# Two memory chains and a feed-forward layer on one core: where the feed-forward pieces stand, a lag of 6 in place of 8, and weights that stay in SBUF

## Chip, cores, metric

One core of one Trainium2 chip. The metric is the device time of one execution in microseconds (us), the median over several executions. The kernels were run in sets, each beside the kernel before on the same chip.

## The reference

Four layers on a sequence of 2048 rows of 448: attention with a carried memory (A), a gated feed-forward layer (B), A again, B again.

```python
x = x + A(layernorm(x));  x = x + B(layernorm(x))
x = x + A(layernorm(x));  x = x + B(layernorm(x))

# A: 64 segments of 32 rows, one after the other
for s in range(64):
    h = concat([mem, xs])                    # 8 memory rows + 32 rows
    q, k, v = h Wq, h Wk, h Wv               # 16 heads of 256
    p = softmax(mask(q k^T / 16))
    o = (p v) Wo
    mem, out = o[:8], o[8:]                  # the memory rows go to the next segment
# B: relu(x Wgate) * (x Wup), then Wdown; inner width 1792
```

The memory makes A serial: 64 segments, each after the other. The kernel runs the two A layers as two chains, the second LAG segments behind the first. One pass of the loop is a **step**: one segment of each chain. Steps in which only one chain runs are single steps, the others double. Both B layers are cut into tiles of 128 rows (four segments), 16 per chain.

## The kernel before

Wq Wk^T and Wv Wo are multiplied out per head at the start (M_sb, B_sb). A step is then: M product (G), scores with a mask, softmax, three value products, attention, and the turn of eight memory rows per chain into the next step's input. Parts (cuts marked):

```python
LAG = 8
# --- in a step: mask, half of the scores, mask, half of the scores
for bb in range(2):
    nc.tensor.matmul(S_ps[RR, bb, 0:8 * L], ident[RR, RR], maskbB[RR, :, :], start=True, ...)
    for sl in range(NSL):
        for c in chains:
            ...  nc.tensor.matmul(o, q_T, rhs, start=False, ...)
# ... softmax, value products, attention into AT_ps ...
# --- memory rows of both chains: ScalarE, then a copy on GpSimd, then five small transposes
for c in chains:
    nc.scalar.copy(mb[m_lo:m_hi, 0:DM], AT_ps[m_lo:m_hi, 0:DM])
    nc.gpsimd.tensor_copy(mb[m_lo:m_hi, 512:576], mb[m_lo:m_hi, 384:448])
    for kd in range(NSL):
        nc.tensor.transpose(MT_ps[:, kd, :], mb[m_lo:m_hi, lo:lo + 128], ...)
    set_memT(c, MT_ps[:, :, :], s + 1)

# --- layer norm: 12 small VectorE operations (Newton) for 1/sqrt, ScalarE scales
# --- feed-forward: tiles of both chains as a pair (N=256); weights come by DMA for each pair
for i, f in enumerate(range(f_lo, f_hi)):
    load_dm_rows(nc.sync if i % 2 == 0 else nc.gpsimd, wg, B_W_gate[:, f * 128:(f + 1) * 128])
    ...
# --- and stands in four chunks at the ends of steps
add_fill(base + 1, lambda pair=pair: ffn_chunk(pair, 0))
add_fill(base + 2, lambda pair=pair: ffn_chunk(pair, 1))
...
for g in range(nsteps):
    chain_step(g, chains, vox_tiles)
    for fn in fill[g]: fn()
```

## Time and profile before

| | |
|---|---|
| device time, 4 runs | 2062.09 us (2057.74 to 2063.97) |
| steps | 8 single, 56 double, 8 single |
| TensorE busy | 93% of the span |
| mean granted TensorE clock | 0.979 |
| read from HBM | 64.92 MB |

Four double steps and the feed-forward work of one pair make a **block**, some 115 us, and the kernel before spends 1610 us in 14 of them: the block is the thing to read.

### The profile page before, as it was taken

To read this page: it belongs to the slowest core of one execution; us is meant where nothing else is said; L and a number is where in the kernel's file an instruction comes from. 1 tells how busy PE (TensorE), PEld (TensorE's weight loads), DVE (VectorE), ACT (ScalarE), POOL (GpSimd) and SP (SyncE) were. 2 spreads that over 40 slices of the span, in tenths; PEclk is the share of its full clock that TensorE was granted. 3 is DMA by queue.
4 is the path that set the end of the run, shared out by engine and by line. 5 is a ranking of instruction groups with operands and counts; after the bars stand their busy time and mean duration, and the time that the engine had idled before them with its cause. 6 is when DMAs were issued, how large, how long until landed. Compare 5 with 4: busy or idle time off the path is not lost.

```text
span 2058.8 us, 79459 instructions
## 1 busy us (share of the span) xinstructions
PE 1916.8 (93%) x35590; PEld 1429.8 (69%) x35590; DVE 1237.5 (60%) x3406; ACT 663.5 (32%) x1429; POOL 457.8 (22%) x1223
## 2 busy tenths in 40 slices
PE   4799999999999999999999999999999999999997
PEld 1377777776767776676767776676767676776764
DVE  3645656666665656656665656656665656665543
ACT  2423332333333332333333332333333332333232
POOL 1201331121303130131303130131303130132232
PEclk9899999999999999999999999999999999999998
DMA  9500210020202020020102020020102020011121
GB/s 257 107 5 21 48 47 21 23 49 20 50 9 52 16 56 16 20 52 20 47 9 54 16 54 18 20 51 20 47 7 56 14 54 15 22 48 28 42 56 42
DMA packets 199541, 82.91 MB, mean 40 GB/s; under 512 B 177120, under 2 KB 191136, under 8 KB 199200
## 3 DMA queue, kind: packets, MB, share of 16 engines
q1 hardware_dynamic: 168240, 43.04, 9.4%
q0 software_dynamic: 20160, 28.93, 5.5%
q10 hardware_dynamic: 10800, 5.86, 1.0%
q8 instruction: 278, 4.55, 0.9%
q14 instruction: 63, 0.52, 0.1%
HBM read 64.92 MB, written 1.84 MB: 32 GB/s over the span
## 4 chain that ended last, share of the span: by engine, by line
PE 83%; DVE 8%; ACT 4%; issue 2%; DMA 1%; POOL 0%; SPq 0%; POOLq 0%; ACTq 0%; DVEq 0%
PE ps L255 30%; PE ps L379 22%; PE AT_ps L455 6%; PE gps L322 5%; PE ups L322 5%; PE S_ps L407 4%; PE dps L334 4%; ACT mb L465 2%; PE bps L115 2%; PE PT_ps L441 1%; PE MT_ps L470 1%; DVE G L390 1%; DVE x_ring L475 1%; ACT xn L218 1%; DVE stats L191 1%
## 5 line engine op out<-in xcount | busy, mean ns | idle before, releaser
L379 PE MATMUL ps<-hT,M_sb 128*128 128x80 bf16 (+1 forms) x16128 | 558.2, 198 | 19.8 <-DVE hT L241 18.1
L379 PEld LDWEIGHTS <-M_sb 128*128 128x128 bf16 x16128 | 555.2, 100 | 25.9 <-issue 22.0
L255 PE MATMUL ps<-B_sb,hT 128*32 128x448 bf16 x8192 | 419.8, 353 | 0.0
L255 PEld LDWEIGHTS <-hT 128*32 128x32 bf16 x8192 | 268.5, 96 | 114.7
L265 DVE CAST vox<-ps 128x448 bf16<-128x448 f32 x512 | 300.4, 620 | 41.8 <-PE ps L255 16.5
L390 DVE CAST G<-ps 128x160 bf16<-128x160 f32 (+1 forms) x312 | 184.7, 595 | 219.1 <-PE ps L379 218.9
L388 ACT CAST G<-ps 128x480 bf16<-128x480 f32 (+1 forms) x328 | 178.6, 549 | 390.3 <-PE ps L379 390.3
L466 POOL COPY mb<-mb 8x64 bf16<-8x64 bf16 x126 | 29.1, 231 | 1108.0 <-ACT mb L465 1108.0
L255 PE MATMUL ps<-B_sb,memT_padP 128*32 128x448 bf16 x4608 | 239.8, 353 | 0.0
L255 PEld LDWEIGHTS <-memT_padP 128*32 128x32 bf16 x4608 | 145.0, 96 | 69.0
L263 ACT CAST VOm<-ps 128x448 bf16<-128x448 f32 x288 | 139.9, 528 | 162.7 <-PE ps L255 162.5
L327 DVE SCALAR_TENSOR_TENSOR hh<-gps,ut 128x128 bf16<-128x128 f32 x448 | 111.9, 286 | 133.8 <-ACT ut L325 131.8
L322 PE MATMUL gps<-xnT,wg 128*128 128x256 bf16 (+1 forms) x1008 | 153.6, 275 | 18.4 <-DVE xnT L313 13.3
L465 ACT CAST mb<-AT_ps 8x448 bf16<-8x448 f32 x126 | 65.9, 523 | 286.0 <-PE AT_ps L455 284.7
L475 DVE TENSOR_TENSOR x_ring<-AT_ps,x_ring 32x448 bf16<-32x448 f32 x128 | 79.1, 618 | 122.5 <-ACT mb L465 118.7
L322 PE MATMUL ups<-xnT,wu 128*128 128x256 bf16 (+1 forms) x1008 | 148.8, 273 | 1.3 <-DMA wu<-in_B_W_up_dram 1.1
L325 ACT CAST ut<-ups 128x256 bf16<-128x256 f32 (+1 forms) x252 | 87.8, 348 | 155.1 <-PE ups L322 147.1
L407 PE MATMUL S_ps<-G,hT 128*40 128x320 bf16 (+1 forms) x1280 | 104.5, 275 | 19.2 <-ACT G L388 19.2
L413 DVE TENSOR_REDUCE mx<-S_ps 104x16 f32<-104x640 f32 (+1 forms) x72 | 59.3, 824 | 103.5 <-PE S_ps L407 103.5
L322 PEld LDWEIGHTS <-wg 128*128 128x128 bf16 x1008 | 93.4, 102 | 33.6 <-issue 19.6
L322 PEld LDWEIGHTS <-wu 128*128 128x128 bf16 x1008 | 96.6, 103 | 15.4 <-DMA wu<-in_B_W_up_dram 1.3
L455 PEld LDWEIGHTS <-PT 128*40 128x40 bf16 x1024 | 54.8, 99 | 75.0 <-issue 39.8
(80 smaller groups left out, 1942.0 us busy)
## 6 DMA issues: line engine op xcount, KB each, us to landing
wg<-in_B_W_gate_dram SPq DMA_DIRECT2D x126, 96.0 KB, 2.5
wu<-in_B_W_up_dram SPq DMA_DIRECT2D x126, 96.0 KB, 2.5
wu<-in_B_W_up_dram POOLq DMA_DIRECT2D x126, 96.0 KB, 2.7
wg<-in_B_W_gate_dram POOLq DMA_DIRECT2D x126, 96.0 KB, 3.0
wo<-in_A_Wo_dram ACTq DMA_DIRECT2D x4, 896.0 KB, 6.5
wg<-in_B_W_gate_dram SPq DMA_DIRECT2D x126, 16.0 KB, 2.4
wu<-in_B_W_up_dram SPq DMA_DIRECT2D x126, 16.0 KB, 2.6
wu<-in_B_W_up_dram POOLq DMA_DIRECT2D x126, 16.0 KB, 2.5
```

The lines of the kernel that those rows point to most:

```text
L255: nc.tensor.matmul(ps[32 * hq:32 * hq + 32, 0:DM], lhsT_fn(kd), B_sb[:, kd, h * DM:(h + 1) * DM], start=(kd == 0), stop=(kd == KDT - 1), t ...
L263: nc.scalar.copy(dst[:, g, :], ps[:, 0:DM])
L265: nc.vector.tensor_copy(dst[:, g, :], ps[:, 0:DM])
L322: nc.tensor.matmul(ps[:, 0:N2], W_sb[:, kd, :], pair.xnT2[:, kd, 0:N2], start=(kd == 0), stop=(kd == KDT - 1))
L327: nc.vector.scalar_tensor_tensor(out=task.hh[:, f, :], in0=gps[:, 128 * i:128 * (i + 1)], scalar=0.0, in1=ut[:, 128 * i:128 * (i + 1)], op ...
L379: nc.tensor.matmul(ps[:, mi * NP:(mi + 1) * NP], M_sb[:, kd, (t0 + mi) * 128:(t0 + mi + 1) * 128], hTP[:, j, kd, c_lo:c_lo + NP], start=(k ...
L388: nc.scalar.copy(dst, src)
L390: nc.vector.tensor_copy(dst, src)
L407: nc.tensor.matmul(o, q_T, rhs, start=False, stop=(sl == NSL - 1), tile_position=(0, c.rb), skip_group_check=True)
L455: nc.tensor.matmul(at_tiles[c.cid][c.rb:c.rb + L, 0:DM], PT[:, gg, c.rb:c.rb + L], rhs, start=(gg == 0), stop=(gg == 7), tile_position=(0, ...
L465: nc.scalar.copy(mb[m_lo:m_hi, 0:DM], AT_ps[m_lo:m_hi, 0:DM])
L475: nc.vector.tensor_tensor(xrows, AT_ps[c.rb:c.rb + SEG, 0:DM], xrows, op=ALU.add)
```

## The change

The intent: keep TensorE occupied in the waits of a step, and drop steps, reloads and side work.

- Feed-forward per tile (N=128), cut into pieces (turn, seven gate-and-up products of 16 matmuls, down), in a queue; hooks put pieces after the M product (mid), before chain 2's value product (late), before the memory transposes (end) and after them (post).
- LAG 6: 70 steps, 12 single and 58 double.
- Gate and up weights loaded once. Tails of the 448-wide contraction share 128-row tiles, which frees the room for it.
- Both masks ahead of the scores; memory rows of chain 2 leave through VectorE while ScalarE does chain 1's.
- 1/sqrt of the layer norm by an addition and a power on GpSimd; the scaling after it moves from ScalarE to VectorE.
- Loads of wo, Wd and x moved to SyncE's queue.

The core of the diff, cut:

```diff
-LAG = 8
+LAG = 6
 ...
-            nc.scalar.dma_start(wo[:], WoF[:, 8 * i:8 * (i + 1), :])
+            nc.sync.dma_start(wo[:], WoF[:, 8 * i:8 * (i + 1), :])
 ...
+    for i, w in enumerate((B_W_gate, B_W_up)):
+        nc.sync.dma_start(Wgu[:, :, i, :], w[0:384].rearrange("(k p) n -> p k n", p=P))
+        nc.sync.dma_start(WguT[64 * i:64 * i + 64, :], w[384:448])
 ...
-        for _ in range(3):                       # Newton, on VectorE
-            ...
+        nc.gpsimd.tensor_scalar(out=rstd[:], in0=mv[:, 1:2], scalar1=EPS, scalar2=None, op0=ALU.add)
+        nc.gpsimd.tensor_tensor(out=rstd[:], in0=rstd[:], in1=mhalf[:], op=ALU.pow)
 ...
+        mid()
         for bb in range(2):
             nc.tensor.matmul(S_ps[RR, bb, 0:8 * L], ident[RR, RR], ...)
+        for bb in range(2):
             r4 = slice(4 * bb, 4 * bb + 4)
             ...
-                nc.scalar.copy(mb[m_lo:m_hi, 0:DM], AT_ps[m_lo:m_hi, 0:DM])
-                nc.gpsimd.tensor_copy(mb[m_lo:m_hi, 512:576], mb[m_lo:m_hi, 384:448])
+            (cp_a if c is chains[0] else cp_v)(mb[rows, 0:DM], at[c.cid][rows, 0:DM])
+        end()
         ...                                      # memory transposes
+        post()
 ...
+        if r == 0:                               # r: step number modulo 4
+            def mid():
+                fill(0, 3)
+            def end():
+                prep_ln(C1, gb + 2)
+                fill(0, 1)
+            def post():
+                fill(0, 1)
 ...
```

## The prediction

> **What bounds the kernel now.** I read the page's busy table first, then its chain of work, then a table of windows over the steady part, then the TensorE timeline of that part.
>
> ```profile
> span 2058.8 us, 79459 instructions
> PE 1916.8 (93%) x35590; PEld 1429.8 (69%) x35590; DVE 1237.5 (60%) x3406; ACT 663.5 (32%) x1429; POOL 457.8 (22%) x1223
> ...
> PE 83%; DVE 8%; ACT 4%; issue 2%; DMA 1%; POOL 0%; SPq 0%; POOLq 0%; ACTq 0%; DVEq 0%
> ```
>
> TensorE is busy 93% of the span and carries 83% of the chain that ended last. So two things count: how much TensorE work there is, and the 7% where it stands. The kernel has 72 steps: eight with chain 1 alone, 56 with both chains, eight with chain 2 alone. Four double steps and one pair of feed-forward tiles make a block; a typical one by windows (columns: length, then PE, PEld, DVE, ACT, POOL busy, clock, DMA share, GB/s):
>
> ```profile
> 906.00:1022.08 116.08, 110.74 (x2047) 83.56 (x2046) 73.02 (x206) 37.33 (x79) 25.32 (x69) 0.99 0.13 32
> ```
>
> TensorE stands 5.3 us in 116.1; no other engine is over two thirds busy. The timeline of one double step, with two later waits:
>
> ```profile
> 1027.21 8.19 PE L379 MATMUL ps<-hT,M_sb 128*128 128x80 bf16 x224
> 1035.33 0.73 PE L407 MATMUL S_ps<-G,hT 128*40 128x320 bf16 x10
> ...
> 1036.91 3.25 PE L255 MATMUL ps<-B_sb,memT_padP 128*32 128x448 bf16 x64
> 1039.95 3.24 PE L255 MATMUL ps<-B_sb,hT 128*32 128x448 bf16 x64
> 1043.12 0.36 PE L441 MATMUL PT_ps<-ident,Px 104*128 104x104 bf16 x4
> ...
> 1043.59 3.25 PE L255 MATMUL ps<-B_sb,hT 128*32 128x448 bf16 x64
> 1046.77 1.19 PE L455 MATMUL AT_ps<-vox,PT 128*40 128x448 bf16 x8
> ...
> 1049.21 0.80 PE L470 MATMUL MT_ps<-ident,mb 8*128 8x8 bf16 x9 [0.23 <-ACT mb L465]
> ...
> 1051.79 8.19 PE L379 MATMUL ps<-hT,M_sb 128*128 128x80 bf16 x224 [1.17 <-DVE hT L241]
> ...
> 1062.62 0.73 PE L407 MATMUL S_ps<-G,hT 128*40 128x320 bf16 x10 [1.73 <-ACT G L388]
> ```
>
> Differences of starts give the true cost, because durations overlap: M product 8.12, scores 1.58, two value products 6.21, transposes of P 0.47, third value product 3.18, attention 1.87, mask and memory transposes about 1.15. Sum 22.6 us of TensorE work per double step. The same reading of a single step (starts at 118.85 and 136.21 of the M product, 17.36 apart, waits 0.67 and 0.39 and their latencies taken off) gives 16.1.
>
> **What the Trainium skill says.** "TensorE: Matmul & The Clock Gate", section "Wait — 56ns, not 53.3ns?": warm matmuls start N/2.4 + 2.5 ns apart, 55.6 ns at N=128. Its section "Back-to-back issue gap" instead says about 81 ns at N=128 where each has its own weight load. It matters, because the change halves N in the gate and up products. The trace has N=128 groups of four, each with its own weights:
>
> ```profile
> 2038.20 0.63 PE L322 MATMUL gps<-xnT,wg 128*128 128x128 bf16 x4
> 2038.62 0.63 PE L322 MATMUL ups<-xnT,wu 128*128 128x128 bf16 x4
> ...
> 2041.16 0.39 PE L322 MATMUL ups<-xnT,wu 128*128 128x128 bf16 x4
> 2041.38 0.39 PE L322 MATMUL gps<-xnT,wg 128*128 128x128 bf16 x4
> ...
> 2045.66 0.34 PE L322 MATMUL ups<-xnT,wu 128*128 128x128 bf16 x3 [0.90 <-DMA wu<-in_B_W_up_dram]
> ```
>
> Starts 0.22 us apart per four: 56 ns, so the first section holds and the 81 do not. The 0.42 per four at 2038 is the cold clock of that page's section "What you observe": about half rate for some 3.4 us after idleness; here it lasted from 2037.4 to 2040.2. "DMA: Bandwidth & Descriptors", "Latency and other measured facts", gives 261 GB/s for a DMA transpose; here one of 0.92 MB held the queue for 3.9 us, 235 GB/s. "GPSIMD Engine Reference", "Elementwise — side-by-side cycle accounting", has two-input work on GpSimd about twice as slow as on VectorE; the change puts the power of the layer norm there, and no row of this trace has that operation.
>
> **The change part by part.** It is a rewrite; I built it and read its instruction order.
>
> *Unchanged.* The contraction of 448 still takes four matmuls: the tails of two heads now share a 128-row tile that meets a zeroed half of the input. That frees memory, not TensorE time. 224 + 64 + 64 (+64) matmuls per step stay.
>
> *Added on TensorE.* Gate and up run per tile at N=128. One pair before: 14 x 2 x 0.436 = 12.2 us; after: 2 x 14 x 2 x 0.223 = 12.5. Down stays 2.65 per tile. With 0.35 of transposes a tile costs 9.26.
>
> *Removed off the path.* The reload of gate and up weights for each of 18 pairs (GpSimd's and SyncE's queues) and 12 Newton operations of about 0.155 us per layer norm on VectorE. They free engines that were not the bound; their worth is in the waits.
>
> *Moved: the fillers.* Before, feed-forward work stood only at the ends of steps, in large chunks. Now pieces of 16 matmuls (0.89 us) stand after the M product (covers the eviction of G, the 1.73), between attention and the memory transposes (covers the mb eviction), and after these (covers the hT copies, the 1.17). The built order shows them there in three of four steps, and a down product of 2.65 in the fourth. VectorE's order has the x_ring addition of chain 1 ahead of the hT copies, so PSUM frees in time.
>
> *Fewer steps.* A lag of 6 gives 12 single and 58 double steps: content 12 x 16.1 + 58 x 22.6 = 1504 against 16 x 16.1 + 56 x 22.6 = 1523. 19 us of TensorE work less, and four partly empty single steps less.
>
> Now the clock from start to end, in us.
> - Start: first M product at 100.6 before. The first weight product began at 21.4 because two wo loads, Wd and x competed with the first transposes (10.1 and 7.2 us on the queue instead of 3.9). All these now follow in SyncE's queue: about 12. Twelve transposes of 3.9, four wo loads of about 3.8 and Wd of 6.6 make it load-bound: I walk the queue to a last product near 81, against 89. The 11.6 us that followed (layer norm, mem0, weights) shrink: both layer norms are scheduled early; the zeroing of the 16-slot input ring on GpSimd remains, 3.5 in all. Start 84.5.
> - Six single steps: four of 17.4, two with content 16.1, one feed-forward tile 9.3, transposes 1.1, leftover waits 0.5: 112.7. At 197.
> - 58 double steps: 58 x 22.6 = 1309 (22.58 unrounded), 27.7 feed-forward tiles x 9.26 = 256.5, 27 input transposes x 0.37 = 10: 1575.5. A block before had content 109.1 and took 116.1: 5.3 gaps and 1.7 of slower clock and tails. I leave 2.0 and 1.0 of these per block, x 14.5 = 43.5. Sum 1619. At 1816.
> - Six single steps: 96.6, two tiles and a down product 21.2, transposes 1.2, waits 3: 122. At 1938.
> - Last tile alone: before, 2030.7 to 2058.8, with the gate and up products stretched from 6.3 to 14 us by weight loads (the 0.90 above). After: addition 0.9, layer norm 2.4, turn 1.5, products cold at first 7.6, last eviction and down 3, addition 0.9, store 2.4: 18.7. At 1957.
>
> Device times lie about 2 us over the span (2060.7 for the profiled 2058.8): **1959 us**, 5% faster.
>
> **Rivals.** (1) *The waits move instead of going.* For it: in the second step of each block a down product, an addition, statistics, GpSimd's two operations and the scaling must run in 5 us beside chain 2's value evictions, and VectorE is strictly in order; a slow power on GpSimd (2 us) would stall those evictions and the attention matmuls. Against it: once per block. If the gaps stay at 5 per block: 1959 + 45 = 2004. (2) *Another engine becomes the bound.* ScalarE takes over half the vox evictions and one more small copy per chain; VectorE loses some 8 us per block of Newton work and four small evictions' overhead per pair. By counts times durations ScalarE has about 12 and VectorE about 15 us in a 28 us step: no. (3) *N=128 runs at 81 ns.* 32 x 112 x 25 ns = 90 us more: 2049, about equal. The trace speaks against it. (4) *No gaps left and full clock:* 1575 in the middle: 1915. (5) *The prelude gains nothing*, loads being serial on one queue: 1973.
>
> **Range and chances.** The sum's largest terms are the gaps (2 per block could be 0.5 to 4: -22 to +29) and the start (plus or minus 8). 1925 to 1993. The 2% border lies at 2021, beyond rival 1: faster 0.95, same 0.04, slower 0.01.
>
> **What would show it.** Right: N=128 groups at 0.22 per four; blocks of about 112; no wait of TensorE on weights by DMA after the start; the first M product near 85; the last tile in about 19 us. Wrong: TensorE waits over 1 us on vox, PT or hT in the second step of a block; GpSimd operations of the layer norm over 1 us each; a first M product after 95; a lower granted clock than 0.98 under the denser load.

## The result, and the profile after

| | before | after |
|---|---|---|
| median | 2063.02 us (13 runs, 2057.74 to 2065.81) | 1874.48 us (8 runs, 1873.02 to 1878.06) |
| ratio | | 0.909, 95% interval 0.9082 to 0.9099 |
| mean granted clock | 0.979 | 0.995 |

A ratio is the mean time of one kernel's fast runs over that of the other's in the same rounds, so it isn't quite the ratio of the medians. All outputs are right. The time lies 85 us below the predicted 1959 and 51 below the range. Two lines of the page's busy table and the chain of work by engine, after:

```profile
span 1871.5 us, 77734 instructions
PE 1820.2 (97%) x36594; PEld 1398.2 (75%) x36594; DVE 1002.0 (54%) x2028; ACT 725.3 (39%) x1563; POOL 79.4 (4%) x276
...
PE 92%; DVE 3%; DMA 2%; SPq 1%; POOL 1%; issue 1%; ACT 0%; POOLq 0%; ACTq 0%
```

TensorE is now 97% busy and carries 92% of the chain. By stage, cut at the starts of the M products of the two traces (the last tile at the end of the last step):

| stage | before | predicted | after |
|---|---|---|---|
| to the first M product | 100.6 | 84.5 | 80.8 |
| single steps, chain 1 | 149.5 (8) | 112.7 (6) | 116.5 (6) |
| double steps | 1609.8 (56) | 1619 (58) | 1531.1 (58) |
| single steps, chain 2 | 170.8 (8) | 122 (6) | 126.1 (6) |
| last tile | 28.1 | 18.7 | 17.0 |

Four of the five stages came within 4.2 us of the working. The miss is one row, 88 us in the double steps. A block there takes 106.3 us, where the prediction's sign of being right was about 112. A block of each kernel by windows (columns: length, then PE, PEld, DVE, ACT, POOL busy, clock, DMA share, GB/s), first one of before that is a little quicker than the typical one:

```profile
1027.21:1141.91 114.70, 109.35 (x2048) 82.98 (x2047) 73.03 (x206) 37.33 (x79) 25.32 (x68) 1.00 0.14 33
```

and one of after:

```profile
1040.92:1147.24 106.32, 106.24 (x2161) 83.06 (x2160) 59.17 (x120) 41.83 (x90) 4.62 (x17) 1.00 0.02 5
```

Idle time fell from 5.35 us to 0.08. But *busy* time fell too, from 109.35 to 106.24, though the A matmuls are the same in number and feed-forward matmuls are more (N halved). Busy time that can shrink without work going away was not all work. Part of the timeline of one double step after (start, length, engine, group):

```profile
1127.19 0.44 PE L217 MATMUL tps<-ident,xn 128*128 128x128 bf16 x5
1127.47 0.44 PE L331 MATMUL S_ps<-maskb,ident 104*104 104x320 bf16 x2
1127.84 1.27 PE L343 MATMUL S_ps<-G,hTr 128*40 128x320 bf16 x20
...
1142.56 1.09 PE L389 MATMUL AT_ps<-VOm,PT 128*40 128x448 bf16 x8
1143.58 0.45 PE L217 MATMUL tps<-ident,xn 128*128 128x128 bf16 x5
1143.87 0.44 PE L331 MATMUL S_ps<-maskb,ident 104*104 104x320 bf16 x2
1144.24 0.41 PE L402 MATMUL tps<-ident,mb 8*128 8x8 bf16 x10
1144.58 2.82 PE L267 MATMUL dps<-Wd_sb,hh 128*128 128x448 bf16 x14
```

No line carries a wait in brackets. From start to start, two masks take 0.37 us and the ten memory transposes 0.34. The same boundary before, with the second mask further on:

```profile
1048.64 0.34 PE L395 MATMUL S_ps<-maskbB,ident 104*104 104x320 bf16 x1
...
1050.16 0.17 PE L470 MATMUL MT_ps<-ident,mb 8*128 8x8 bf16 x1
...
1060.56 0.34 PE L395 MATMUL S_ps<-maskbB,ident 104*104 104x320 bf16 x1
```

One mask alone takes 0.57 from its start to that of the first memory transpose (1049.21, shown in the prediction), of which the profile names 0.23 as a wait. Nine memory transposes then last 0.74 until the next group at 1049.95, with no wait in brackets, where after needs 0.34 for ten. Part of this wait stands in rows that the reading above leaves out, those of TensorE's weight loads (PEld), since mb is loaded as weights here. Of the kernel before:

```profile
1049.21 0.16 PEld L470 LDWEIGHTS <-mb 8*128 8x128 bf16 x4 [0.44 <-ACT mb L465]
1049.57 0.35 PEld L470 LDWEIGHTS <-mb 8*128 8x128 bf16 x5 [0.20 <-POOL mb L466]
```

The second of them waits for GpSimd's copy of 64 columns, which the change removes. Over the whole trace the weight loads of the memory transposes wait 51.7 us for evictions and copies before, and 10.5 after.

I summed such start-to-start differences over one block by kind of matmul (a wait falls to the group before it; sums are the block lengths):

| us per block | before | after | all_undone (below) |
|---|---|---|---|
| M product | 32.47 | 32.10 | 32.40 |
| value products | 37.56 | 37.57 | 37.57 |
| gate and up | 12.35 | 13.04 | 12.52 |
| down | 5.30 | 5.41 | 5.38 |
| scores | 5.25 | 5.24 | 5.84 |
| attention | 7.49 | 7.35 | 7.92 |
| transposes of P | 1.88 | 1.78 | 1.79 |
| masks, and what follows | 5.16 | 1.48 | 3.73 |
| input and feed-forward transposes, and what follows | 3.89 | 1.23 | 2.94 |
| memory transposes, and what follows | 3.35 | 1.12 | 2.60 |
| sum | 114.70 | 106.32 | 112.69 |

All of the gain, 8.57 of 8.38 us, is in the last three kinds: the boundaries of a step. The typical block before takes 116.1 us, another 1.4. Those are in its gate and up products, 13.73 instead of 12.35. In the timeline of such a block:

```profile
962.09 1.01 PE L322 MATMUL gps<-xnT,wg 128*128 128x256 bf16 x4 [1.02 <-DVE xnT L313]
962.90 1.06 PE L322 MATMUL ups<-xnT,wu 128*128 128x256 bf16 x4
...
965.23 0.60 PE L322 MATMUL gps<-xnT,wg 128*128 128x256 bf16 x4
```

Four matmuls take 0.81 to 0.86 from 962.09 to 964.6, then 0.44: half clock for 2.5 us right after the waits. Over the 12 blocks from 302 to 1692 us the step that holds this stretch lasts 29.88 in two of them and 31.27 to 32.36 in ten, a mean excess of 1.39 us per block, some 19 us in all (14 blocks). After's clock is 1.00 in every 200 us of the double steps from 400 to 1600, and its blocks there agree within 0.01 us.

### The profile page after: what moved, and what is told of

It reads as the page before. It is cut to its first block, busy times and chain, and to the rows that moved or that the text cites.

```text
span 1871.5 us, 77734 instructions
## 1 busy us (share of the span) xinstructions
PE 1820.2 (97%) x36594; PEld 1398.2 (75%) x36594; DVE 1002.0 (54%) x2028; ACT 725.3 (39%) x1563; POOL 79.4 (4%) x276
## 4 chain that ended last, share of the span: by engine, by line
PE 92%; DVE 3%; DMA 2%; SPq 1%; POOL 1%; issue 1%; ACT 0%; POOLq 0%; ACTq 0%
PE ps L293 31%; PE ps L321 29%; PE gu L257 11%; PE AT_ps L389 6%; PE S_ps L343 5%; PE dps L267 5%; PE PT_ps L379 2%; PE ps L123 1%; PE S_ps L331 1%; PE tps L217 1%; SPq L109 1%; PE tps L402 1%; DVE vox L295 1%; DMA wq<-in_A_Wq_dram 1%; DVE stats L201 1%; DMA wo<-in_A_Wo_dram 1%
## 5 line engine op out<-in xcount | busy, mean ns | idle before, releaser
L321 PE MATMUL ps<-hTr,M_sb 128*128 128x80 bf16 (+1 forms) x11760 | 542.2, 198 | 10.6 <-DVE hTr L405 4.9
L321 PE MATMUL ps<-hTr,MT_sb 128*128 128x80 bf16 (+1 forms) x3920 | 537.4, 198 | 0.0
L293 PE MATMUL ps<-B_sb,hTr 128*32 128x448 bf16 x6144 | 392.2, 353 | 0.0
L321 PEld LDWEIGHTS <-MT_sb 128*128 128x128 bf16 x3920 | 388.9, 99 | 0.0
L293 PEld LDWEIGHTS <-hTr 128*32 128x32 bf16 x8192 | 267.3, 96 | 117.2 <-issue 5.2
L324 DVE CAST G<-ps 128x480 bf16<-128x480 f32 x314 | 186.2, 594 | 254.5 <-PE ps L321 253.3
L257 PE MATMUL gu<-xnT,Wgu 128*128 128x128 bf16 x2688 | 218.8, 219 | 1.0 <-ACT xnT L246 0.7
L293 PE MATMUL ps<-B_sb,memTp 128*32 128x448 bf16 x3360 | 216.4, 355 | 0.0
L293 PE MATMUL ps<-BT_sb,hTr 128*32 128x448 bf16 x2048 | 206.4, 352 | 0.0
L257 PEld LDWEIGHTS <-Wgu 128*128 128x128 bf16 x2688 | 183.3, 98 | 25.9 <-issue 22.6
L257 PE MATMUL gu<-xnT,WguT 128*128 128x128 bf16 x896 | 196.0, 219 | 0.5 <-DVE xnT L247 0.5
```

The lines of the kernel that those rows point to most:

```text
L257: nc.tensor.matmul(ps[:, i, ff], w, self.xnT[:, kd if kd < 3 else 3 + i], start=(kd == 0), stop=(kd == 3))
L293: nc.tensor.matmul(ps[32 * hq:32 * hq + 32, 0:DM], lhsT(kd if kd < 3 else 3 + g4 % 2), w, start=(kd == 0), stop=(kd == 3), tile_position=( ...
L321: nc.tensor.matmul(ps[:, (t - t0) * NP:(t - t0 + 1) * NP], w, hT[:, kd if kd < 3 else 3 + p7 % 2, c0:c1, :], start=(kd == 0), stop=(kd == 3))
L324: (cp_a if bb % 2 == 0 else cp_v)(G[:, t0:t0 + n, c0:c1, :], ps[:, 0:n * NP].rearrange("p (m c t) -> p m c t", m=n, t=L))
```

## The experiments

The theories. **H (hidden waits):** 22.6 us of "content" per step held waits that the busy column of TensorE's matmuls counts as work; the change takes them away with several small parts, and leaves nothing. **F (fillers):** the placement of the feed-forward pieces is the gain, through the named waits. **C (clock):** the half-clock stretches are what was gained. Parts of the change are undone in the changed kernel, alone and together, and two are done alone in the kernel before. Differences below are of medians against 1874.5.

**1. The pieces between attention and the memory transposes, moved to after them.** (Shown for steps 2 and 3 of four; step 0 alike, step 1 has no such piece.)

```diff
             def end():
-                fill(1, 1)
             def post():
-                fill(1, 1)
+                fill(1, 2)
```

> Feed-forward pieces that stood between attention and the memory transposes now stand after these. Theory F (the pieces cover the eviction of the memory rows): TensorE waits about 0.5 us before the memory transposes in three of four double steps, some 43 times, and in the single steps with feed-forward work: about +25 us over the 1874.5 of the changed kernel, 1900. Theory W (the changed kernel simply has less TensorE work per step, wherever the pieces stand): within 5 us of 1874.5.

1888.86 us, ratio to before 0.9169 (0.9155 to 0.9183): 14.4 slower, between W's 5 and F's 25. A block takes 107.4. Idle time in the matmul rows grows by only 4 us; the weight loads of the memory transposes wait 29.3 us for ScalarE's copy, 10.2 in after. So these pieces do cover that copy, for about half of what F had.

**2. The pieces after the M product, moved likewise.** (Shown for step 0.)

```diff
-            def mid():
-                fill(0, 3)
             def post():
-                fill(0, 1)
+                fill(0, 4)
```

> Feed-forward pieces that stood after the M product now stand at the end of the step (or before chain 2's values in the step whose down product follows). Theory F: a wait on G of up to 1.7 us comes back in some steps, about +10 to +20 us: 1885 to 1895. Theory W: within 5 us of 1874.5.

1874.62 us, ratio 0.91 (0.9086 to 0.9113): no difference. The pieces that were to cover the eviction of G, behind the largest named wait before (1.73), do nothing by themselves at a lag of 6.

**3. All pieces to the place after the memory transposes.**

```diff
-            mid, end: fill(...)
+            post: all of the step's pieces (5 in step 0, 5 in step 2, 3 in step 3; 4 in late of step 1)
```

> Both of the two: all pieces at the end of the step, as the kernel before had them, but with the changed kernel's other parts. Theory F in its strong form (the placement is most of the 9.8 us per block): +100 us, 1975. In a weak form (placement is a part; the rest is the parallel eviction of the memory rows and the masks ahead of the scores): +40 us, 1915. Theory W: within 10 us of 1874.5.

1909.87 us, ratio 0.9266 (0.9251 to 0.9281): 35.4 slower, block 108.4. F in its strong form, that placement is the gain, is wrong: it is 35 of 188 us when it alone is undone; its weak form had 40. Numbers 1 and 2 add to 14.5, so some 21 us come only when no piece is left in either place. The wait that returns is not on G but on the feed-forward layer's own input xnT, before its first products, this kernel first, then after:

```profile
L257 PE MATMUL gu<-xnT,Wgu 128*128 128x128 bf16 x2688 | 207.0, 219 | 21.6 <-ACT xnT L246 21.6
L257 PE MATMUL gu<-xnT,Wgu 128*128 128x128 bf16 x2688 | 218.8, 219 | 1.0 <-ACT xnT L246 0.7
```

In numbers 1 and 2 the same group waits 1.2 and 3.6.

**4. Lag of 8.**

```diff
-LAG = 6
+LAG = 8
```

> Lag 8 instead of 6 in the changed kernel: 72 steps, 16 single ones. By the changed trace a single step is about 16.3 us of work plus 1.3 of waits where nothing fills them, a double step 21.5: four single steps more and two double ones fewer, 4 x 17 - 43 = +25 us, 1900. If the lag is worth nothing: 1875.

1899.81 us, ratio 0.9223 (0.921 to 0.9237): 25.3 slower, as expected; blocks mostly take 106.3 to 106.6 as with 6. The lag is worth its steps, 12.6 us each.

**5. Kernel before, memory rows of chain 2 on VectorE.**

```diff
-                nc.scalar.copy(mb[m_lo:m_hi, 0:DM], AT_ps[m_lo:m_hi, 0:DM])
+                (nc.scalar.copy if c is chains[0] else nc.vector.tensor_copy)(mb[m_lo:m_hi, 0:DM], AT_ps[m_lo:m_hi, 0:DM])
```

> The kernel before with one line changed: the memory-row eviction of chain 2 on VectorE, so that it runs beside chain 1's on ScalarE. Hidden-wait theory (what the prediction counted as 22.6 us of content per double step held waits that no row names; the transposes of the second chain's memory rows took 0.73 us at their first matmul instead of some 0.25): about 0.45 us off each of 56 double steps, 25 us: about 2035. Rival (the gap is a latency of TensorE's own, or VectorE, busy in order with other things at that point, brings the copy no sooner): within 5 us of 2060.

2061.55 us, ratio 0.9989 (0.9974 to 1.0005): nothing in the time. H had 25 us here, so in this form it failed. But the trace shows the hidden wait and where its worth went:

```profile
1046.16 0.61 PE L470 MATMUL MT_ps<-ident,mb 8*128 8x8 bf16 x9 [0.23 <-ACT mb L465]
1046.70 0.28 PE L238 MATMUL tps<-ident,xn 128*128 128x128 bf16 x2
...
1074.79 0.60 PE L322 MATMUL gps<-xnT,wg 128*128 128x256 bf16 x4 [1.03 <-DVE xnT L313]
1075.22 0.93 PE L322 MATMUL ups<-xnT,wu 128*128 128x256 bf16 x4
```

Nine transposes take 0.54 us instead of 0.74, and elsewhere 0.48. Three steps of a block became 0.26, 0.15 and 0.25 us shorter, 0.66 together. The step with the gate and up products after a wait became longer, 31.87 instead of 31.18 in the mean of the same 11 blocks: now all 11 have a half-clock stretch (the last line, 0.72 until the next group at 1075.94, against 0.44 at full clock), where two of before's had none. 0.66 gained, 0.69 given back in these 11; the blocks at either end went the other way (30.01 instead of 32.22, 27.90 instead of 29.60), and all 56 double steps took 1605.6 us against 1609.8. The mean clock fell from 0.979 to 0.973, though TensorE waits less.

**6. The same, and both masks ahead of the scores.**

```diff
         for bb in range(2):
             nc.tensor.matmul(S_ps[RR, bb, 0:8 * L], ident[RR, RR], maskbB[RR, :, :], ...)
+        for bb in range(2):
             r4 = slice(4 * bb, 4 * bb + 4)
```

> The same as before_mb2, and both mask matmuls ahead of all scores instead of one ahead of each half. Hidden-wait theory: the second mask took 0.57 us where after has 0.37 for both; 0.2 to 0.5 us more off each of 72 steps, 15 to 35 us below before_mb2: 2000 to 2020. Rival (the mask order only moves the same wait on the softmax to another matmul): the same as before_mb2 within 5 us.

2041.45 us, ratio 0.9902 (0.987 to 0.9933): 20 us below number 5, within H's range of 15 to 35 (its 2000 to 2020 supposed a number 5 at 2035). One line of mask order is worth 1% in the kernel before, at a still low clock (0.972).

**7. Changed kernel, both memory-row evictions on ScalarE.**

```diff
-            (cp_a if c is chains[0] else cp_v)(mb[rows, 0:DM], at[c.cid][rows, 0:DM])
+            cp_a(mb[rows, 0:DM], at[c.cid][rows, 0:DM])
```

> The changed kernel with both memory-row evictions on ScalarE, as before. If the feed-forward piece between attention and the memory transposes covers that eviction: within 4 us of 1874.5. If the parallel eviction itself is what was gained: 0.45 us x 58 = 26 us slower, about 1900.

1879.57 us, ratio 0.911 (0.9092 to 0.9129): 5.1 slower, near the "covered" reading and far from 26. With a piece in front, that eviction hardly counts.

**8. Changed kernel, masks split again.**

```diff
             nc.tensor.matmul(S_ps[RR, bb, 0:8 * L], ident[RR, RR], maskb[RR, :, :], ...)
-        for bb in range(2):
             r4 = slice(4 * bb, 4 * bb + 4)
```

> The changed kernel with the old order mask, half of the scores, mask, half. Hidden-wait theory: 0.2 to 0.5 us per step x 70, 14 to 35 us slower: 1888 to 1910. Rival (the order is only cosmetic once chain 2's softmax is early): within 4 us of 1874.5.

1890.5 us, ratio 0.9169 (0.9146 to 0.9192): 16.0 slower. No engine is waited for; the cost shows only from start to start:

```profile
1030.69 0.30 PE L331 MATMUL S_ps<-maskb,ident 104*104 104x320 bf16 x1
1030.92 0.73 PE L342 MATMUL S_ps<-G,hTr 128*40 128x320 bf16 x10
1031.58 0.34 PE L331 MATMUL S_ps<-maskb,ident 104*104 104x320 bf16 x1
1031.85 0.73 PE L342 MATMUL S_ps<-G,hTr 128*40 128x320 bf16 x10
```

The masks take 0.23 and 0.27, 0.50 together, against 0.37 for two in a row. With the scores that makes 0.2 us per step, 0.8 per block (107.1), all of it booked as busy. Why a mask between two halves of the scores costs more was not taken further.

**9. Newton on VectorE in the changed kernel.** The two GpSimd lines replaced by the operations of before, the loop's twelve and three ahead of it; the scaling stays on VectorE.

```diff
-        nc.gpsimd.tensor_scalar(out=rstd[:], ..., op0=ALU.add)
-        nc.gpsimd.tensor_tensor(out=rstd[:], in0=rstd[:], in1=mhalf[:], op=ALU.pow)
+        for _ in range(3):
+            nc.vector.tensor_tensor(...)   # x4
```

> The changed kernel with the reciprocal square root of the layer norm back on VectorE, as 12 small operations in place of two on GpSimd. If VectorE is off the path (54% busy): within 5 us of 1874.5. If the prediction's worry had a core (layer norm work of some 1.9 us in VectorE's queue ahead of evictions that TensorE waits for): once or twice per block of four steps, 10 to 25 us slower.

1889.18 us, ratio 0.916 (0.9143 to 0.9177): 14.7 slower; the "within 5" that I thought likelier missed. The groups of TensorE's transposes of layer-normed rows, this kernel first:

```profile
L230 PE MATMUL tps<-ident,xn 128*128 128x128 bf16 x320 | 28.7, 221 | 17.3 <-DVE xn L222 17.3
```

then after:

```profile
L217 PE MATMUL tps<-ident,xn 128*128 128x128 bf16 x320 | 28.7, 221 | 5.3 <-DVE xn L209 5.3
```

12 us more of waiting for VectorE, though that engine is only 59% busy: 5.0 of them are 0.36 at one place of each block (which grew by 0.5); 6.9 are in three waits where no other work stands between a layer norm and its transposes: 3.52 instead of 0.97 in the last single step of chain 1, 5.48 and 3.24 instead of 3.56 and 0.81 in the tail. A share of busy time says nothing of a latency.

**10. The loads of wo, Wd and x on ScalarE's queue again.**

```diff
-            nc.sync.dma_start(wo[:], WoF[:, 8 * i:8 * (i + 1), :])
+            nc.scalar.dma_start(wo[:], WoF[:, 8 * i:8 * (i + 1), :])   # likewise Wd, x
```

> The changed kernel with the loads of wo, Wd and x on ScalarE's queue again, so that they run beside the first transposes. The prediction's working: the first weight product at 21.4 instead of 12, the first M product some 9 us later, so about 1883. Rival (the front is bound by the sum of all loads, in whatever order they come): within 3 us.

1884.94 us, ratio 0.914 (0.9123 to 0.9158): 10.5 slower. The first weight product of this kernel:

```profile
17.27 6.68 PE L123 MATMUL ps<-wq,wk 128*128 128x448 bf16 x20 [9.47 <-DMA wq<-in_A_Wq_dram]
```

and of after (counts and lengths are cut by the window asked for):

```profile
12.08 4.08 PE L123 MATMUL ps<-wq,wk 128*128 128x448 bf16 x13 [6.86 <-DMA wq<-in_A_Wq_dram]
```

The first M product follows at 94.2 instead of 80.8. The prediction's working of the front held in size, though it had 21.4 where 17.27 was measured. In the traces of the kernels with after's loads it comes at 80.8 to 84.6, so differences of a few us in the front say nothing.

**11. Lag of 5**, with the hooks moved so that chain 2's inputs are ready a step earlier.

```diff
-LAG = 6
+LAG = 5
```

> The changed kernel with a lag of 5 in place of 6: 69 steps, 10 single and 59 double; the places of the fillers are moved so that chain 2's inputs are ready a step earlier. From the lag of 8 being 25 us slower (12.6 us per step of lag): 1862. If the shorter lag makes TensorE wait for chain 2's layer norm and transposes in every block: 1875 or more.

1866.43 us, ratio 0.9048 (0.9029 to 0.9068): 8.0 faster than after, the fastest kernel, against 12 expected. The block is unchanged (106.33), so chain 2 doesn't make TensorE wait; the missing 4 us are at the ends, not looked into (the front is 2.2 us later in the profiled run, within its scatter).

**12. Six parts undone together**: numbers 3, 4, 7, 8, 9 and 10 (five of the schedule, and the loads).

> The changed kernel with five parts of the schedule undone together: fillers only after the memory transposes, both memory-row evictions on ScalarE, masks split, lag of 8, Newton on VectorE, and the loads of wo, Wd and x on ScalarE's queue. If the parts simply add: 1874.5 + 35 + 5 + 16 + 25 + what newton_dve and loads_on_act cost (0 to 10 each) = 1956 to 1975. If the parts cover each other (an uncovered wait exposes the next, and gaps bring back the slow clock): 1985 to 2020, with a mean granted clock below 0.985. What is left up to 2060 is then the reload of the feed-forward weights and the pairs' chunks.

2029.52 us, ratio 0.9841 (0.982 to 0.9862): 155.0 slower than after, more than the range for covering parts. The parts alone add to 35.4 + 25.3 + 5.1 + 16.0 + 14.7 + 10.5 = 107.0; so 48 us exist only together. The window of one block without half clock:

```profile
813.81:926.50 112.69, 108.20 (x2161) 83.91 (x2160) 63.91 (x178) 44.32 (x94) 1.73 (x8) 1.00 0.02 5
```

Both halves of before's loss are back: 4.49 us idle and 1.96 more busy than after's 106.24, with the same instructions on TensorE. Its blocks vary from 112.7 to 116.1, the length of before's, at a mean clock of 0.987 (I had asked for less than 0.985). This is what H says: the same matmuls, more busy time.

**13 to 16. Which parts hide each other**, added one after the other onto number 3: evictions on ScalarE, Newton, both, and the masks as well.

> Fillers only after the memory transposes, and both memory-row evictions on ScalarE. The parts alone cost 35.4 and 5.1 us. If they add: 1915. If the filler had hidden the eviction (TensorE now reaches the transposes while ScalarE still copies the second chain's rows, 0.4 to 0.5 us per step): 0.4 to 0.5 us x 58 over all_to_post, 1933 to 1939.

1928.49 us, ratio 0.9352 (0.9336 to 0.9367): 18.6 over number 3, where the eviction alone cost 5.1. This is a real pair: with no piece ahead of the memory transposes TensorE reaches them before the second copy is done. The transposes' group in this kernel:

```profile
L402 PE MATMUL tps<-ident,mb 8*128 8x8 bf16 x630 | 34.7, 164 | 22.8 <-ACT mb L394 17.8
```

and in after:

```profile
L402 PE MATMUL tps<-ident,mb 8*128 8x8 bf16 x630 | 23.3, 164 | 3.6 <-ACT mb L394 3.3
```

> Fillers only after the memory transposes, and Newton on VectorE. The parts alone cost 35.4 and 14.7 us. If they add: 1925. If VectorE's extra work, some 2.6 us per layer norm, falls into waits that no filler covers now (input transposes, hT copies, G): 1 to 2 us per block over the sum, 1940 to 1954.

1926.81 us, ratio 0.9342 (0.9328 to 0.9355): 16.9 over number 3; Newton alone cost 14.7. These two add.

> The three together. If they add: 1930. If the interaction lies between these: 1950 to 1970, and the block near 111.5. If the interaction belongs to the slow clock, which would need all the gaps: near 1930 to 1940 with a clock as in all_to_post (0.993).

1941.18 us, ratio 0.9412 (0.9398 to 0.9426), between my expectations (1930 to 1940 if clock alone, 1950 to 1970). The block is 109.83, only 0.13 above that of post_mb (109.70), and every block has the same length.

> The whole steady schedule undone, with the lag of 6 and the loads as in the changed kernel. all_undone less the lag's 25.3 and the loads' 10.5: 1994, if these two are independent of the rest. With the mask's 16 added to post_mb_newton: 1966 to 1986. A block of 113 to 114; if slow clock enters here and not in post_mb_newton, its blocks vary in length and the clock is below 0.99.

1981.56 us, ratio 0.9604 (0.959 to 0.9618). Within the range from the mask (1966 to 1986); the 1994 was too high, so lag and loads, undone on top of this, cost 48.0 and not the 35.8 of their sum. The masks cost 40.4 us here and 16.0 alone. The blocks now have three lengths, 111.28, 112.91 and 114.54, in no order: steps of 1.63, and the clock is 0.983 where it was 0.991. Part of the timeline of a long one:

```profile
331.00 0.34 PE L344 MATMUL S_ps<-maskb,ident 104*104 104x320 bf16 x1
331.59 0.28 PE L414 MATMUL tps<-ident,mb 8*128 8x8 bf16 x5 [0.24 <-ACT mb L406]
332.14 0.28 PE L414 MATMUL tps<-ident,mb 8*128 8x8 bf16 x5 [0.27 <-ACT mb L406]
332.34 0.45 PE L230 MATMUL tps<-ident,xn 128*128 128x128 bf16 x5
333.47 0.33 PE L270 MATMUL gu<-xnT,Wgu 128*128 128x128 bf16 x3 [0.67 <-ACT xnT L259]
...
335.18 0.53 PE L270 MATMUL gu<-xnT,Wgu 128*128 128x128 bf16 x3
```

Between 331.0 and 333.5 TensorE has a mask, a few transposes and three waits. A microsecond into the gate and up products, from 334.5 to 337.7, three matmuls take 0.53 in place of 0.33, and the 64 of them last 5.20 us against 3.57 in a block without it. The Trainium skill, "TensorE: Matmul & The Clock Gate", section "What's actually happening", says that the clock follows the activity in a free-running window of about 3.4 us; a half-clock stretch of 3.2 us that comes in some blocks and not in others with the same instructions agrees with that. What decides it in a given block was not shown here.

So of 40.4, by block means: 1.45 per block by the masks themselves (111.28 less 109.83) and 1.34 by half clock (mean of 12 blocks 112.62), times 14.5 blocks. C alone is not the cause: post_mb_newton has all its blocks alike, and one mask's place brings the stretches of half clock, which then add some 20 us. That they need more waiting is not shown: number 5 waits less than before and has more of them.

**The sum.** Of 188 us, 155 go with the six parts: 107 each by itself, 48 only together: 13.5 the pair in post_mb, 24.4 the masks (clock included), 12.2 the lag and the loads, and Newton 2.0 less than alone. Some 32 us (2061.4 in those rounds less 2029.5) were not undone by any kernel: reloads of gate and up weights, pairs at N=256 in large chunks, GpSimd's copies, the layer norm's scaling on ScalarE, the tails of the contraction in tiles of their own. How these divide stays open. In the stages, all_undone is 25 us quicker than before in its 56 double steps, 7 in the front, 10 in the tail and slower by 8 in the first single steps.

## Why the prediction was wrong

- **The direction and most of the mechanisms held.** No transfer is waited for after the start, N=128 groups run at 56 ns a matmul, the last tile takes 17 us (18.7 predicted), the first M product starts at 80.8 (84.5), the fewer steps are worth 25, GpSimd's power takes 0.57 us, and no double step waits for it. None of the rivals but the fourth, "no gaps left and full clock", was near, and its 1915 was still 40 too high. (The fifth's 1973 is a slip: 1959 and the 16.1 of the front make 1975.)
- **The failed step is the content of a double step: "Sum 22.6 us of TensorE work per double step", and with it "58 x 22.6 = 1309".** Its terms "scores 1.58" and "mask and memory transposes about 1.15" come to 2.73 us per step, 10.9 per block. In the changed kernel scores, masks and memory transposes take 5.24 + 1.48 + 1.12 = 7.84 us per block. The 3.1 us between them were not work that had to stay: waits that the matmul lines show without a bracket, and the cost of a mask between two halves of the scores, whose nature is open. mask_split, post_mb and all_undone bring such time back without adding a matmul. Over 14.5 blocks: 45 us.
- **The second term is the allowance: "I leave 2.0 and 1.0 of these per block, x 14.5 = 43.5".** Idle time is 0.08 us per block and no half clock is left. The prediction took the named gaps to be separate leftovers, each to be covered partly. How much of that is chaining can be bounded only: all_undone costs 48 us more than its parts apart.
- 45 and 43.5 make 88.5, and the double steps came out 88 us shorter than the working. The other stages together moved it by 3.
- **"Pieces ... after the M product (covers the eviction of G, the 1.73)" is not borne out at a lag of 6**: mid_to_post costs nothing, and no wait on G comes back even with all pieces at the end. It returns only in all_undone, which differs from post_mb_mask_newton, where there is none, by the lag of 8 and the loads; lag8, where pieces still stand after the M product, has none either. So it takes the lag of 8 together with another undone part; whether that is the missing piece was not tested. The groups of the scores in all_undone and after:

```profile
L355 PE MATMUL S_ps<-G,hTr 128*40 128x320 bf16 (+1 forms) x1280 | 107.7, 277 | 21.0 <-DVE G L337 21.0
L343 PE MATMUL S_ps<-G,hTr 128*40 128x320 bf16 (+1 forms) x1280 | 97.1, 275 | 0.0
```

- **"They free engines that were not the bound; their worth is in the waits"** was right in words and not in the sum: the Newton operations are worth 14.7 us alone, and no term of the prediction held them.

The Trainium skill, "Perfetto Trace Analysis", section "Tensor Engine Instruction (MATMUL, LD_WEIGHTS)", says that a matmul's end is estimated and not observed. No run here shows the true ends, but the busy sums fit that: 2048 matmuls in 109.35 busy us before, 2161 in 106.24 after. I had taken the differences of starts as "the true cost"; a difference of starts is work only if nothing was waited for in between, and for short groups at the boundary of a step that can't be read from one kernel.

## What to carry to other kernels

Where the next group starts is what TensorE lost, not what the busy column or a bracket says: read the rows of the weight loads too, measure small groups (a mask, ten tiny transposes) against the least that the same group takes anywhere, and count the rest as a wait that can go. When an engine is near 95% busy with several small gaps, try the cures together: one alone can be given back in part by the next gap or by the clock (2061.6 against 2064.0 in the same rounds), while six undone at once cost 155 us and not the 107 that they cost one by one. And the order of two small matmuls, both masks ahead of the scores, was worth 16 to 20 us, as much as larger pieces of the rewrite.

## What the Trainium skill lacked or had wrong

- "TensorE: Matmul & The Clock Gate", section "Back-to-back issue gap": about 81 ns per matmul at N=128 with a weight load each. The changed kernel runs 16 of them in 0.90 us, 56 ns, as the same page's section "Wait — 56ns, not 53.3ns?" has it.
- The same page on the slow clock: its practical rule is about gaps of some 3 us. It also tells of short idles between groups, without a length or a count for them. In the double steps here the longest wait is 2.4 us (all_undone), and in post_mb_mask_newton it is 1.0; there a stretch of 2.5 us with a mask, 15 transposes and waits of 0.24, 0.27 and 0.67 was followed, 1 us later, by 3.2 us at half rate, 1.63 us lost each time.
- "Perfetto Trace Analysis", on busy time: it calls it a bad measure, but not how far it goes. Here the same A matmuls and more feed-forward matmuls had 3.1 us less busy time per block of 106 to 115 us.
- No page gives a time for a power on GpSimd: on 128x1 elements it took 567 ns, the addition before it 222 (spans on GpSimd are rough in these profiles).
